# A pruned linear layer: seven tiles of x turned on TensorE instead of eight, the eighth's first half of K opened from natural weights and staged, weight pieces 2 and 3 by rows

## Chip, cores, metric

One core of a Trainium2 chip. The metric is the device time of one launch in microseconds, median over runs; the profile is of one further execution.

## The reference

x is 16 x 512 x 1024, w 1024 x 1024, b 1024, all bf16. Rows of w are taken in groups of four (M = 4), and in each group and column the two of the largest magnitude are kept (N = 2):

```python
wg = w.reshape(G, M, D)
mag = jnp.abs(wg)
order = jnp.argsort(mag, 1)
thr = jnp.take_along_axis(mag, order[:, M - N:M - N + 1, :], 1)
mask = (lambda x, dt: x.astype(dt))(mag >= thr, w.dtype)
wp = (wg * mask).reshape(D, D)
return jnp.einsum("bsd,df->bsf", x, wp) + b
```

## The kernel before

x is 8192 tokens, 64 tiles of 128 tokens (t = 0 to 63). K = 1024 is cut in two halves (g = 0, 1) of 512 rows. Output columns are cut in two halves (h) of FH = 512, and those in quarters (n) of CW = 256.

**Two layouts of the weights.** w is loaded with the four rows of a group side by side (`w_sb`: partition q, half g, row m of the group, column), since pruning compares those four. VectorE prunes it in six *pieces*: 0 to 3 are the four column quarters of the first half of K, 4 and 5 the two column halves of the second. Each piece goes through `abs`, `hi` and `lo` (maximum and minimum of two rows), `t1`, `t2`, `thr`, `mask` (L154) and `mult`, which writes `wp`. A letter behind a step cuts it: x and y are the row pairs m = 0, 1 and m = 2, 3; u, v, s, t are one m each. Pieces 0 and 1 are cut by rows in `mask` and `mult` (`halves`), 2 to 5 are whole. Once a column half of a K half is pruned, SBUF to SBUF DMAs (`spread`, token `W g.h`, four parts of 128 KB) write it in natural row order to `wp_nat`, which all later tiles use.

**Packed tiles.** While `wp_nat` isn't there yet, TensorE works on the first eight tiles (NPK = 8) with `wp` itself. The first half of K of each is loaded plainly (`load_x`, token rows interleaved by GROUPS), turned on TensorE with a stride of four (`transpose`, T tokens, four instructions of 128 x 128 each), copied to SBUF by ScalarE (`copy_xt`, C tokens) and multiplied in `mm_piece` (M t.piece, L216): 256 columns for one m. Two tiles share a PSUM bank per column quarter (`pairs`); ScalarE copies each full bank to a staging tile (`stage`, S tokens).

**Natural tiles.** All other tiles come by transposing DMAs: `load_lead` (X0, X1: the two K halves of tiles 8 to 11, LEAD = 4), `load_low` (Y1, Y0: the second K half of the packed tiles, in two groups of 384 and 640 rows) and `load_nat` (the batches of 4 and then 8 tiles, both K halves). They are multiplied in `nat` (L239): 512 columns for one of eight blocks kt of K. The lead tiles open with K blocks 0 to 3 (`open_nat`, A j h), and their PSUM banks are held until the second K half of the weights is there.

**Closes.** Then the list `closes` runs: for each (t, h), K blocks 4 to 7, an eviction on VectorE that adds the bias (L400) or the staged first half, to which GpSimd has added the bias (L402, L396), and a store when both halves are done. GpSimd's eight additions begin when the last piece is pruned. After the closes come 52 tiles of the main loop, 16 natural matmuls each.

**Order.** Every engine's instructions are chained in program order (`seq`), and up to the closes that order is written out by hand as four lists of tokens (`order`: pe, dve, act, sp). An engine thus stops at a token whose input is late, with all that stands behind it. PSUM has two banks for `tp` and six for `ps`. The fillers (F and the ones before) are matmuls on constants ahead of the first transposes.

Of the kernel before, what the change touches and what calls it, by code (L numbers as in the profile page):

```python
# [10 lines left out]
def kernel(  # L11
# [25 lines left out]
    xf = x.flatten_outer_dims()  # L37
    of = out.flatten_outer_dims()

    NPK = 8  # L40
    LEAD = 4
    GROUPS = ((0, 5), (5, 8))
    LATE = 5
    sizes = (4, 8, 8, 8, 8, 8, 8)
    batches = []
# [6 lines left out]
    const = ctx.enter_context(tc.tile_pool(name="const", bufs=1))  # L52
    wtmp = ctx.enter_context(tc.tile_pool(name="wtmp", bufs=1))
    xtp = ctx.enter_context(tc.tile_pool(name="xtp", bufs=NPK))
    stg = ctx.enter_context(tc.tile_pool(name="stg", bufs=NPK))
    xtb = ctx.enter_context(tc.tile_pool(name="xtb", bufs=2))
    outp = ctx.enter_context(tc.tile_pool(name="outp", bufs=10))
    psum_t = ctx.enter_context(tc.tile_pool(name="psum_t", bufs=2, space=bass.MemoryType.PSUM))
# [52 lines left out]
    load_w(0, 0, 256, 1, 2, "act")  # L111
    load_w(0, 0, 256, 2, 3)
    load_w(0, 0, 256, 3, 4, "act")
    load_x(7, 8, "act")
    load_x(0, 2, "act")
    act(nc.scalar.activation(spark[:], nc.const_aps.tensor(1.0, [P, 1], bf16), Act.Abs))
    load_x(5, 7)
    load_w(0, 256, 512)
    load_x(4, 5)
    load_x(2, 4)  # L120
    load_w(0, 512, 1024)
    load_w(1, 0, 512)
    sp(nc.sync.dma_start(bias_sb[:], b.partition_broadcast(P)))
    load_w(1, 512, 1024)
    pieces = [(0, 0, 256), (0, 256, 512), (0, 512, 768), (0, 768, 1024), (1, 0, 512), (1, 512, 1024)]

# [56 lines left out]

    def transpose(t):
        xg = x_sb[t].rearrange("p (q m) -> p m q", m=4)
        bank = psum_o.tile([P, FH], fp32, name="ps") if t == 6 else psum_t.tile([P, FH], fp32, name="tp")
        tp = bank[:].bitcast(bf16)[:, :FH].rearrange("p (m q) -> p m q", m=4)
        for m in range(4):
            pe(nc.tensor.transpose(tp[:, m, :], xg[:, m, :], ident[:]))  # L189
        xpk[t] = tp  # L190
# [7 lines left out]
    part = {"": slice(0, 4), "x": slice(0, 2), "y": slice(2, 4), "a": slice(0, 2), "b": slice(2, 4)}  # L198
    part.update({c: slice(m, m + 1) for m, c in enumerate("uvst")})
    half = {"a": slice(0, 1), "b": slice(1, 2)}  # L200
    pairs = [(5, 6), (0, 1), (2, 3), (4, 7)]
    pair_of = {t: q for q, pr in enumerate(pairs) for t in pr}
    left = {}

    def mm_piece(t, i, ms):
        g, c0, c1 = pieces[i]
        q, n = pair_of[t], c0 // CW
        new = (q, n) not in ps_open
        if new:
            ps_open[(q, n)] = psum_o.tile([P, FH], fp32, name="ps")  # L210
            left[(q, n)] = sum(8 for pc in pieces if pc[0] == 0 and pc[1] // CW == n)
        ps = ps_open[(q, n)]
        d = pairs[q].index(t) * CW - n * CW
        for m in range(ms.start, ms.stop):
            left[(q, n)] -= 1
            pe(nc.tensor.matmul(ps[:, c0 + d:c1 + d], lhsT=xpk[t][:, m, :],  # L216
                                rhs=wp[:, g, m, c0:c1],
                                start=(new and m == ms.start), stop=(left[(q, n)] == 0),
                                skip_group_check=True))

    xlead = const.tile([P, KT, LEAD * P], bf16)
# [15 lines left out]
    def nat(xt, ps, c0, c1, k0=0, k1=KT, first=0, last=KT - 1, koff=0):  # L237
        for kt in range(k0, k1):
            pe(nc.tensor.matmul(ps, lhsT=xt[:, kt - koff, :], rhs=wp_nat[:, kt, c0:c1],  # L239
                                start=(kt == first), stop=(kt == last)))  # L240

    def open_nat(j, h):
        t = NPK + j
        if j < 3:
            held[(t, h)] = psum_o.tile([P, FH], fp32, name="ps")
        else:
            held[(t, h)] = psum_t.tile([P, FH], fp32, name="tp")
        nat(xnat[t], held[(t, h)][:], h * FH, (h + 1) * FH, 0, 4)

    staged = {}  # L250

    def stage(q, n):
        if (q, n // 2) not in staged:
            staged[(q, n // 2)] = stg.tile([P, 2, 2, CW], fp32, name="st")
        st = staged[(q, n // 2)]
        act(nc.scalar.copy(st[:, n % 2, :, :].rearrange("p t c -> p (t c)"), ps_open.pop((q, n))[:]))  # L256

    order = {
        "pe": (
            "F8 T7a T5a T6a M7.0u M5.0u M7.0v M5.0v M6.0u M6.0v M7.0s M5.0s T1a M7.0t M5.0t M6.0t M6.0s "  # L260
            "T0a M1.0u M1.0v M1.0s M1.0t T4a T3a M0.0u M0.0v M0.0s M0.0t T2a M4.0u M4.0v M4.0s M4.0t "
            "M3.0u M3.0v M3.0s M3.0t M2.0u M2.0v M2.0s M2.0t M4.1x M5.1x M0.1x M7.1y M6.1y M2.1y M1.1y "
            "M3.1y M6.1x M4.1y M1.1x M3.1x M0.1y M7.1x M2.1x M5.1y M0.2 M3.2 M7.2 M1.2 M2.2 M4.2 M6.2 "
            "M0.3 M2.3 M5.3 M4.3 M5.2 M6.3 M3.3 M1.3 A0h0 A2h0 M7.3 A2h1 A1h0 A3h1 A0h1 A3h0 A1h1"
        ),
        "dve": (
            "abs0a hi0a abs0b lo0a lo0b hi0b t20 t10 thr0 mask0u mask0v mult0u mult0v mask0s mask0t mult0s mult0t abs1 lo1 hi1 "
            "t21 t11 thr1 mask1x mask1y mult1x mult1y abs2 hi2 lo2 t12 t22 thr2 mask2 mult2 hi3 lo3 "
            "t13 t23 thr3 mask3 mult3 abs5 abs4 hi4 lo4 t24 t14 thr4 mask4 mult4 hi5 lo5 t15 t25 "
            "thr5 mask5 mult5"  # L270
        ),
        "act": (
            "C7a C5a C6a C1a C0a C4a C3a C2a S3b0 S0b0 S1b0 S2b0 abs3 S3b1 S1b1 S0b1 S2b1 S2b2 S1b2 "
            "S3b2 S0b2 S1b3 S2b3 W1.0q S3b3 S0b3"
        ),
        "sp": (
            "W0.0 X0 X1 W0.1 Y1 W1.0p Y0 W1.1"
        ),
    }
    written = set()  # L280
    p = {}
    halves = {0: tuple("uvst"), 1: ('x', 'y')}

    by_rows = {0}

# [9 lines left out]
    def needs(eng, tok):  # L295
        base, k = split_tok(tok)
        if tok[0] == "C":
            return ["T" + tok[1:]]
        if tok[0] == "T":
            return ["C" + transposed[-2]] if tok != "T6a" and len(transposed) > 1 else []  # L300
        if tok[0] == "F":
            return []
        if tok[0] == "W":
            g, h = map(int, tok[1:4].split("."))
            return [n for i, pc in enumerate(pieces) if pc[0] == g and pc[1] // FH == h for n in all_of(f"mult{i}", i)]
        if tok[0] in "XY":
            return []
        if tok[0] == "A":
            return ["X0", f"W0.{tok.split('h')[1]}"]
        if base[0] == "M":  # L310
            t, i = base[1:].split(".")
            return [f"C{t}a", f"mult{i}{k}"]
        if tok[0] == "S":
            q, n = map(int, tok[1:].split("b"))
            return [f"M{t}.{x}" for i, pc in enumerate(pieces) if pc[0] == 0 and pc[1] // CW == n
                    for t in pairs[q] for x in all_of(str(i), i)]
        i, step = base[-1], base[:-1]
        before = {"abs": [], "hi": ["abs"], "lo": ["abs"], "t1": ["hi"], "t2": ["lo"],
                  "thr": ["t1", "t2"], "mask": ["thr", "hi", "lo"], "mult": ["mask"]}[step]
        out_ = []  # L320
        for b_ in before:
            if b_ in ("abs", "hi", "lo") and int(i) in by_rows:
                out_ += [b_ + i + k] if step in ("hi", "lo") else [b_ + i + s for s in "ab"]
            else:
                out_.append(b_ + i + (k if b_ == "mask" else ""))
        return out_

    def emit(eng, tok):
        base, k = split_tok(tok)
        if tok[0] == "T":  # L330
            transpose(int(tok[1:-1]))
            if tok != "T6a":
                transposed.append(tok[1:])
        elif tok[0] == "F":
            filler(int(tok[1:]))
# [4 lines left out]
            xnat.update(load_lead(int(tok[1:])))  # L340
        elif tok[0] == "Y":
            xnat.update(load_low(int(tok[1:])))
        elif tok[0] == "A":
            open_nat(*map(int, tok[1:].split("h")))
        elif tok[0] == "C":
            copy_xt(int(tok[1:-1]))
        elif tok[0] == "M":
            mm_piece(*map(int, base[1:].split(".")), part[k])
        elif tok[0] == "S":
            stage(*map(int, tok[1:].split("b")))  # L350
        else:
            i = int(base[-1])
            if i not in p:
                p[i] = Piece(i)
            if eng == "act":
                p[i].abs_act()
            else:
                p[i].do(base[:-1], part[k], half.get(k, slice(0, 2)))
# [27 lines left out]

    pruned = const.tile([P, 1], bf16)
    pool(nc.gpsimd.tensor_copy(out=pruned[:], in_=wp[:, 1, 3, Dout - 1:]))
    closes = [(8, 0), (9, 0), (10, 0), (11, 0), (5, 0), (6, 0), (7, 0), (8, 1), (9, 1), (10, 1), (11, 1), (5, 1), (6, 1), (7, 1), (4, 0), (4, 1), (0, 0), (0, 1), (1, 0), (1, 1), (2, 0), (2, 1), (3, 0), (3, 1)]
    done = set()  # L390
    for t, h in closes:
        if t < NPK and (pair_of[t], h) not in done:
            done.add((pair_of[t], h))
            st = staged[(pair_of[t], h)]
            bias = bias_sb[:, h * FH:(h + 1) * FH].rearrange("p (n c) -> p n c", n=2)
            pool(nc.gpsimd.tensor_tensor(st[:], st[:], bias[:, :, None, :].to_broadcast([P, 2, 2, CW]), op=Alu.add))  # L396

    def evac(o, ps, c0, c1, add=None):
        if add is None:
# [17 lines left out]
    def close(t, h):  # L417
# [2 lines left out]
        ps = held.pop((t, h), None)  # L420
        if ps is None:
            ps = psum_o.tile([P, FH], fp32, name="ps")
        nat(xnat[t], ps[:], h * FH, (h + 1) * FH, 4, 8, first=4 if t < NPK else 0, koff=4 if t < NPK else 0)
        add = None
        if t < NPK:
            add = staged[(pair_of[t], h)][:, :, pairs[pair_of[t]].index(t), :]
        evac(outs[t], ps[:], h * FH, (h + 1) * FH, add)
        closed[t] = closed.get(t, 0) + 1
        if closed[t] == 2:
# [61 lines left out]
```

## Time and profile before

| what | value |
|---|---|
| median of three runs | 233.23 us (233.18 to 233.81) |
| the profiled execution | 232.96 us, span 231.2 us |
| TensorE busy | 226.7 us (98%) |
| VectorE busy | 107.8 us (47%) |
| ScalarE, GpSimd busy | 13.5 us, 17.6 us |
| DMA | 38.19 MB, mean 165 GB/s |
| first transpose, first packed matmul | 4.95, 5.88 us after the span's start |
| first natural matmul | 20.68 us |
| first close | 28.03 us |

Times of instructions count from the start of the span; 1.8 us of the profiled execution lie around the span. PE is TensorE, PEld its weight loads, DVE VectorE, ACT ScalarE, POOL GpSimd, SP SyncE; a q behind an engine's name is its queue, where DMAs are issued. L numbers are lines of the kernel before. In a row with x2 or x4, consecutive instructions of one kind are merged, so its length runs from the first start to the last end. The end of a matmul is modelled, so starts are compared.

### The profile page before, as it was taken

The page shows a single profiled execution, that of the slowest core. Times are in us where ns is not written, and L with a number is a line of the kernel's source. Part 1 is how long each engine was busy: PE and PEld are TensorE (multiplying, and loading weights), DVE is VectorE, ACT ScalarE, POOL GpSimd, SP SyncE. Part 2 cuts the span into 40 slices and gives each one's busy share as a digit, 9 for nine tenths or more (in the row PEclk, how much of TensorE's full clock was granted, in tenths as well). Part 3 has the DMA queues.
Part 4 walks back from the last instruction along what each step waited for, and adds up shares of the span by engine and source line. Part 5 has one row for each costly group of instructions (what it writes and reads, how often), then busy time and mean ns, then how long its engine had stood idle before and what let it go on. Part 6 is the DMA issues. An engine that isn't in the chain of part 4 may idle for free.

```text
span 231.2 us, 2832 instructions
## 1 busy us (share of the span) xinstructions
PE 226.7 (98%) x1139; PEld 112.6 (49%) x1158; DVE 107.8 (47%) x188; ACT 13.5 (6%) x27; POOL 17.6 (8%) x15
## 2 busy tenths in 40 slices
PE   8999999999999999999999999999999999999995
PEld 5887444544444444444444444444444444444443
DVE  4999777844424424424424424424423423433434
ACT  3674100000000000000000000000000000000000
POOL 1000299600000000000000000000000000000000
DMA  6999999998499222991249821798129942122122
GB/s 195 357 218 236 228 165 250 265 203 252 183 221 261 110 91 66 244 281 61 78 122 237 231 94 68 167 190 238 67 91 188 247 155 84 55 91 87 57 86 91
DMA packets 78268, 38.19 MB, mean 165 GB/s; under 512 B 63664, under 2 KB 70576, under 8 KB 78256
## 3 DMA queue, kind: packets, MB, share of 16 engines
q1 hardware_dynamic: 67328, 20.61, 45.4%
q10 hardware_dynamic: 10928, 17.40, 21.9%
q8 instruction: 9, 0.15, 0.3%
q14 instruction: 3, 0.02, 0.0%
HBM read 3.41 MB, written 16.78 MB: 87 GB/s over the span
## 4 chain that ended last, share of the span: by engine, by line
PE 96%; DVE 1%; DMA 1%; issue 1%
PE ps L239 88%; PE ps L216 6%; PE tp L239 1%; DMA w_sb<-in_w_dram 1%; PE tp L189 0%; DVE hi L154 0%; DVE lo L154 0%; DVE mag L164 0%; DVE mag L154 0%; DVE o L400 0%; DVE wp L154 0%
## 5 line engine op out<-in xcount | busy, mean ns | idle before, releaser
L239 PE MATMUL ps<-wp_nat,xb 128*128 128x512 bf16 (+2 forms) x832 | 178.9, 375 | 0.8
L239 PEld LDWEIGHTS <-xb 128*128 128x128 bf16 x848 | 82.4, 98 | 97.5
L400 DVE TENSOR_TENSOR o<-ps,bias_sb 128x512 bf16<-128x512 f32 (+1 forms) x112 | 71.6, 677 | 114.2 <-PE ps L239 111.9
L396 POOL TENSOR_TENSOR st<-st,bias_sb 128x1024 f32<-128x1024 f32 x8 | 16.8, 2132 | 0.0
L216 PE MATMUL ps<-wp,xt 128*128 128x256 bf16 x128 | 15.1, 273 | 0.1
L239 PE MATMUL ps<-wp_nat,xlow 128*128 128x512 bf16 x62 | 14.0, 379 | 0.1
L216 PEld LDWEIGHTS <-xt 128*128 128x128 bf16 x128 | 12.2, 98 | 2.0 <-ACT xt L194 0.4
L402 DVE TENSOR_TENSOR o<-ps,st 128x512 bf16<-128x512 f32 x16 | 11.1, 692 | 2.8 <-PE ps L239 2.1
L239 PE MATMUL ps<-wp_nat,xlead 128*128 128x512 bf16 x47 | 11.1, 379 | 0.1
L239 PEld LDWEIGHTS <-xlow 128*128 128x128 bf16 x64 | 7.2, 112 | 6.7
L239 PEld LDWEIGHTS <-xlead 128*128 128x128 bf16 x64 | 6.3, 98 | 7.1
L256 ACT COPY st<-ps 128x512 f32<-128x512 f32 x16 | 8.4, 595 | 6.2 <-PE ps L216 3.7
L154 DVE TENSOR_TENSOR mag<-mag,hi 128x256 bf16<-128x256 bf16 (+3 forms) x10 | 5.6, 582 | 0.2
L154 DVE TENSOR_TENSOR wp<-w_sb,mag 128x256 bf16<-128x256 bf16 (+3 forms) x10 | 5.6, 581 | 0.1
L133 PE MATMUL ps<-const-bfloat16-1.0 128*128 128x128 bf16 (+1 forms) x22 | 4.3, 394 | 0.8 <-PEq L475 0.8
L239 PE MATMUL tp<-wp_nat,xlead 128*128 128x512 bf16 x16 | 4.1, 379 | 0.0
L164 DVE TENSOR_SCALAR mag<-w_sb 128x512 uint16<-128x512 uint16 (+2 forms) x6 | 2.7, 466 | 2.9 <-DMA w_sb<-in_w_dram 2.9
L133 PEld LDWEIGHTS <-const-bfloat16-1.0 128*128 128x128 bf16 x22 | 2.5, 148 | 2.4 <-issue 2.4
L154 DVE TENSOR_TENSOR hi<-mag 128x512 bf16<-128x512 bf16 (+2 forms) x7 | 3.2, 459 | 0.1
L154 DVE TENSOR_TENSOR lo<-mag 128x512 bf16<-128x512 bf16 (+2 forms) x7 | 3.1, 456 | 0.0
L194 ACT COPY xt<-tp 128x256 f32<-128x256 f32 x7 | 2.4, 375 | 3.1 <-PE tp L189 3.1
L189 PE MATMUL tp<-ident,x 128*128 128x128 bf16 x28 | 2.4, 219 | 0.0
(17 smaller groups left out, 14.1 us busy)
## 6 DMA issues: line engine op xcount, KB each, us to landing
out_dram<-o ACTq DMA_DIRECT2D x59, 256.0 KB, 2.5
wp_nat<-wp SPq DMA_DIRECT2D x14, 128.0 KB, 3.4
w_sb<-in_w_dram SPq DMA_DIRECT2D x3, 512.0 KB, 6.6
out_dram<-o ACTq DMA_DIRECT2D x8, 128.0 KB, 1.7
x<-in_x_dram SPq DMA_DIRECT2D x2, 256.0 KB, 4.0
w_sb<-in_w_dram SPq DMA_DIRECT2D x1, 256.0 KB, 4.6
x<-in_x_dram ACTq DMA_DIRECT2D x1, 256.0 KB, 3.7
bias_sb<-in_b_dram SPq DMA_DIRECT2D x1, 256.0 KB, 6.6
```

Source lines behind the costliest of these rows:

```text
L133: pe(nc.tensor.matmul(warm_ps[:, :rep * P], lhsT=nc.const_aps.tensor(1.0, [P, P], bf16), rhs=nc.const_aps.tensor(1.0, [P, rep * P], bf16), ...
L154: dve(nc.vector.tensor_tensor(out, a, b_, op=op))
L164: dve(nc.vector.tensor_single_scalar(self.mag[:, ms, :].bitcast(u16), self.w[:, ms, :].bitcast(u16), 0x7FFF, op=Alu.bitwise_and))
L189: pe(nc.tensor.transpose(tp[:, m, :], xg[:, m, :], ident[:]))
L194: act(nc.scalar.copy(xt[:].bitcast(fp32), xpk[t].bitcast(fp32)))
L216: pe(nc.tensor.matmul(ps[:, c0 + d:c1 + d], lhsT=xpk[t][:, m, :], rhs=wp[:, g, m, c0:c1], start=(new and m == ms.start), stop=(left[(q, n) ...
L239: pe(nc.tensor.matmul(ps, lhsT=xt[:, kt - koff, :], rhs=wp_nat[:, kt, c0:c1], start=(kt == first), stop=(kt == last)))
L256: act(nc.scalar.copy(st[:, n % 2, :, :].rearrange("p t c -> p (t c)"), ps_open.pop((q, n))[:]))
L396: pool(nc.gpsimd.tensor_tensor(st[:], st[:], bias[:, :, None, :].to_broadcast([P, 2, 2, CW]), op=Alu.add))
L400: dve(nc.vector.tensor_tensor(o[:, c0:c1], ps, bias_sb[:, c0:c1], op=Alu.add))
L402: dve(nc.vector.tensor_tensor(o[:, c0:c1].rearrange("p (n c) -> p n c", n=2), ps.rearrange("p (n c) -> p n c", n=2), add, op=Alu.add))
```

## The change

Seven tiles are packed (0 to 6), the lead has five (7 to 11), so the transposed loads X0 and X1 take 640 rows instead of 512, and the second halves of K come in groups of 512 (Y0) and 384 rows (Y1). Tile 7 is between the two kinds: its first half of K is opened with natural weights for each column half (E0, E1: `open_solo`, four natural matmuls into a `tp` bank), and staged by ScalarE (U7h0, U7h1); its close then goes like that of a packed tile. Tile 0 has no partner in a bank any more: it takes a bank of 512 columns for itself per column half (U0h0, U0h1), and shares its staging tile with tile 7. The number of staging copies (16) and of GpSimd's additions (8) stays.

The order is written anew for all four engines. On TensorE pieces 2 and 3 are taken by rows (2u, 2v, 2y; 3x, 3y), as VectorE now ends them, and E0 and E1 stand among the openings. On VectorE `abs5` comes after piece 4 and not before it. On SyncE the bias load moves from the initial loads to behind W0.1, W0.1 moves ahead of X1, and Y0 ahead of W1.1. Eight closes for column half 0 instead of seven precede the first for column half 1.

```diff
-    NPK = 8
-    LEAD = 4
-    GROUPS = ((0, 5), (5, 8))
+    NPK = 7
+    LEAD = 5
+    STG = 8
+    SOLO = 0
+    GROUPS = ((0, 4), (4, 7))
...
-    load_x(7, 8, "act")
-    load_x(0, 2, "act")
+    load_x(6, 7, "act")
+    load_x(0, 1, "act")
...
-    load_x(5, 7)
+    load_x(4, 6)
     load_w(0, 256, 512)
-    load_x(4, 5)
-    load_x(2, 4)
+    load_x(3, 4)
+    load_x(1, 3)
     load_w(0, 512, 1024)
     load_w(1, 0, 512)
-    sp(nc.sync.dma_start(bias_sb[:], b.partition_broadcast(P)))
     load_w(1, 512, 1024)
...
-    pairs = [(5, 6), (0, 1), (2, 3), (4, 7)]
+    pairs = [(4, 5), (SOLO, NPK), (1, 2), (3, 6)]
...
+        if t == SOLO:
+            key, d = (t, "h", c0 // FH), -(c0 // FH) * FH
+        else:
+            key, d = (q, n), pairs[q].index(t) * CW - n * CW
...
+    def open_solo(h):
+        ps = ps_open[(NPK, "h", h)] = psum_t.tile([P, FH], fp32, name="tp")
+        nat(xnat[NPK], ps[:], h * FH, (h + 1) * FH, 0, 4, last=3)
+
     def open_nat(j, h):
-        t = NPK + j
+        t = STG + j
...
-    def stage(q, n):
...
+    def stage(key):
+        solo = key[1] == "h"
+        q, h, at = (pair_of[key[0]], key[2], int(key[0] != SOLO)) if solo else (key[0], key[1] // 2, key[1] % 2)
...
         "pe": (
-            "F8 T7a T5a T6a M7.0u M5.0u M7.0v M5.0v M6.0u M6.0v M7.0s M5.0s T1a M7.0t M5.0t M6.0t M6.0s "
-            "T0a M1.0u M1.0v M1.0s M1.0t T4a T3a M0.0u M0.0v M0.0s M0.0t T2a M4.0u M4.0v M4.0s M4.0t "
-            "M3.0u M3.0v M3.0s M3.0t M2.0u M2.0v M2.0s M2.0t M4.1x M5.1x M0.1x M7.1y M6.1y M2.1y M1.1y "
-            "M3.1y M6.1x M4.1y M1.1x M3.1x M0.1y M7.1x M2.1x M5.1y M0.2 M3.2 M7.2 M1.2 M2.2 M4.2 M6.2 "
-            "M0.3 M2.3 M5.3 M4.3 M5.2 M6.3 M3.3 M1.3 A0h0 A2h0 M7.3 A2h1 A1h0 A3h1 A0h1 A3h0 A1h1"
+            "F8 T6a T4a T5a M6.0u M4.0u M6.0v M4.0v M5.0u M5.0v T0a M6.0s M4.0s M5.0s M6.0t T3a M4.0t M5.0t "
+            "M0.0s M0.0t T2a M3.0v T1a M3.0s M0.0v M0.0u M2.0t M2.0v M2.0u M3.0u M1.0t M1.0v M3.0t M2.0s "
+            "M1.0s M2.1x M3.1x M0.1x M6.1y M4.1y M1.0u M1.1y M2.1y M0.1y M4.1x M1.1x M5.1y M5.1x M6.1x M3.1y "
+            "M3.2u M2.2u M1.2u M6.2u M4.2u M5.2u M0.2u M3.2v M2.2v M1.2v M6.2v M4.2v M5.2v M0.2v M3.2y M2.2y "
+            "M1.2y M6.2y M4.2y M5.2y M0.2y M3.3x M6.3x M5.3x M1.3x M3.3y M6.3y M5.3y M1.3y M4.3x M4.3y M2.3x "
+            "M2.3y M0.3x M0.3y A0h0 E0 A2h0 A1h0 E1 A1h1 A3h0 A2h1 A3h1 A0h1"
         ),
         "dve": (
...
-            "t21 t11 thr1 mask1x mask1y mult1x mult1y abs2 hi2 lo2 t12 t22 thr2 mask2 mult2 hi3 lo3 "
-            "t13 t23 thr3 mask3 mult3 abs5 abs4 hi4 lo4 t24 t14 thr4 mask4 mult4 hi5 lo5 t15 t25 "
-            "thr5 mask5 mult5"
+            "mult0t abs1 lo1 hi1 t21 t11 thr1 mask1x mask1y mult1x mult1y abs2 lo2 hi2 t22 t12 thr2 mask2u "
+            "mask2v mult2u mult2v mask2y mult2y lo3 hi3 t23 t13 thr3 mask3x mult3x mask3y mult3y abs4 hi4 "
+            "lo4 t24 t14 thr4 mask4 mult4 abs5 lo5 hi5 t25 t15 thr5 mask5 mult5"
         ),
         "act": (
-            "C7a C5a C6a C1a C0a C4a C3a C2a S3b0 S0b0 S1b0 S2b0 abs3 S3b1 S1b1 S0b1 S2b1 S2b2 S1b2 "
-            "S3b2 S0b2 S1b3 S2b3 W1.0q S3b3 S0b3"
+            "C6a C4a C5a C0a C3a C2a C1a S3b0 abs3 S0b0 S2b0 U0h0 S2b1 S3b1 S0b1 S3b2 S2b2 S2b3 S0b2 S3b3 "
+            "S0b3 U0h1 U7h0 W1.0q U7h1"
         ),
         "sp": (
-            "W0.0 X0 X1 W0.1 Y1 W1.0p Y0 W1.1"
+            "W0.0 X0 W0.1 B X1 W1.0p Y1 Y0 W1.1"
         ),
...
-    halves = {0: tuple("uvst"), 1: ('x', 'y')}
+    halves = {0: tuple("uvst"), 1: ('x', 'y'), 2: ('u', 'v', 'y'), 3: ('x', 'y')}
...
-    closes = [(8, 0), (9, 0), (10, 0), (11, 0), (5, 0), (6, 0), (7, 0), (8, 1), (9, 1), (10, 1), (11, 1), (5, 1), (6, 1), (7, 1), (4, 0), (4, 1), (0, 0), (0, 1), (1, 0), (1, 1), (2, 0), (2, 1), (3, 0), (3, 1)]
+    closes = [(8, 0), (9, 0), (10, 0), (11, 0), (4, 0), (5, 0), (6, 0), (7, 0), (8, 1), (9, 1), (10, 1), (11, 1),
+              (4, 1), (5, 1), (6, 1), (7, 1), (3, 0), (3, 1), (0, 0), (0, 1), (1, 0), (1, 1), (2, 0), (2, 1)]
```

## The prediction

> **What bounds the kernel now.** I read the page first, then the chain of waits, then the timelines of VectorE and of SyncE's queue, then the tiles of the transposed x.
>
> ```profile
> span 231.2 us, 2832 instructions
> PE 226.7 (98%) x1139; PEld 112.6 (49%) x1158; DVE 107.8 (47%) x188; ACT 13.5 (6%) x27; POOL 17.6 (8%) x15
> ...
> PE 96%; DVE 1%; DMA 1%; issue 1%
> ```
>
> TensorE is busy for 98% and holds 96% of the chain. So time is won only by taking work or a wait from PE, and lost only where PE starts to wait. The chain in order of time (start, length, what):
>
> ```profile
> 5.88 1.19 PE ps L216 x8
> 7.07 0.22 PE tp L189 x4
> ...
> 9.49 11.35 PE ps L216 x104
> 20.85 1.08 PE ps L239 x5
> ...
> 27.33 3.45 PE ps L239 x16
> ```
>
> This gives three prices: a packed matmul (256 columns) 11.35/104 = 0.1092 us, one of the four transposes of a tile 0.0557 (0.22/4), a natural matmul (512 columns) 3.45/16 = 0.2157. From 5.88 to the end no other engine holds the chain for a quarter of a microsecond until the last stores. Inside the first row the eight matmuls start between 5.88 and 6.80, 0.92 us for seven steps of 0.109: gaps of 0.15 us in all, and that is all that PE loses before the natural matmuls. VectorE's timeline, which feeds it:
>
> ```profile
> 9.41 0.75 DVE L154 TENSOR_TENSOR wp<-w_sb,mag 128x512 bf16<-128x512 bf16 x2
> ...
> 12.78 0.69 DVE L154 TENSOR_TENSOR wp<-w_sb,mag 128x1024 bf16<-128x1024 bf16 x1
> ...
> 15.63 0.69 DVE L154 TENSOR_TENSOR wp<-w_sb,mag 128x1024 bf16<-128x1024 bf16 x1
> 16.24 1.29 DVE L164 TENSOR_SCALAR mag<-w_sb 128x2048 uint16<-128x2048 uint16 x2
> ...
> 26.26 1.23 DVE L154 TENSOR_TENSOR wp<-w_sb,mag 128x2048 bf16<-128x2048 bf16 x1
> ```
>
> These are the multiplications that end pieces 1, 2, 3 and the last one (5), and the two absolute values between. SyncE's queue:
>
> ```profile
> 10.19 2.55 SPq L98 DMA_DIRECT2D wp_nat<-wp  x4
> 12.78 4.91 SPq L224 DMA_TRANSPOSE xlead<-in_x_dram  x2
> 17.79 2.49 SPq L98 DMA_DIRECT2D wp_nat<-wp  x4
> ...
> 27.54 3.38 SPq L98 DMA_DIRECT2D wp_nat<-wp  x4
> ```
>
> They are W0.0, X0 and X1, W0.1, and W1.1. And the two tiles, with time from issue to landing:
>
> ```profile
> L224 SPq DMA_TRANSPOSE xlead<-in_x_dram x2: 1628/2430/3233, 12.8 to 16.1; - x2
> ...
> DMA to landing us min/median/max: 4.4/5.0/5.6
> ```
>
> ```profile
> L231 SPq DMA_TRANSPOSE xlow<-in_x_dram x2: 1571/2558/3545, 20.3 to 23.9; - x2
> ...
> DMA to landing us min/median/max: 3.8/5.5/7.1
> ```
>
> X0 (the 5.6) lands at 18.4 and PE wants it at 20.68, the start of its first natural matmul. The 3.5 us and the 7.1 belong to the one transfer of 640 rows.
>
> **PE's work.** Removed: four transposes, 4 x 0.0557 = 0.22, and 16 packed matmuls of the eighth tile, 16 x 0.1092 = 1.75. Added: E0 and E1, 8 natural matmuls, 8 x 0.2157 = 1.73. Sum -0.24 us, all on the path. The bank waits at the start stay: the same three tiles are transposed first, and piece 0 is made by the same instructions.
>
> **PE against VectorE.** From 5.88 come 27 packed matmuls, four transposed tiles (0.22 each) and some 0.10 of start gaps: PE asks for piece 1 at 9.82. Its first half is ready at 9.83, so PE waits some 0.05 there, which uses up what is left of the old 0.15. The third x tile to be transposed late (T3a, at 7.29) needs a load that landed at 7.38 before; 128 KB less of x goes ahead of it, at the 316 to 359 GB/s of those microseconds 0.36 us, so 7.0. If not, 0.1 is lost. Piece 2 is asked for at 9.87 + 29 x 0.1092 = 13.04. By rows its mask and product come as 256 columns for one m: starts 0.21 apart (the row of piece 0, 0.49 for two), so the first product ends at 12.05 + 0.21 x 2 + 0.29 = 12.75. Slack 0.29. Piece 3 is asked for at 13.04 + 28 x 0.1092 = 16.10. Rows cost VectorE some 0.15 more here, yet the half product ends at 16.05 instead of the whole at 16.33: slack 0.05, the whole split being needed. The second half ends at 16.84, asked for at 16.97. So the last packed matmul ends at about 19.2, 1.5 us earlier than PE turned to natural weights before (it has 16 fewer of them in front).
>
> **The transfers now needed earlier.** W0.0 is released by piece 1 as before (10.19) and lands at 16.2: no wait. X0 follows at 12.78 with 640 rows for 512: 128 rows are 131 KB, at the 269 GB/s of that stretch 0.49 us, so it lands at 18.4 + 0.5 = 18.9, while PE wants it at 19.1 to 19.2. That is the thinnest cover of the change, 0.3 us for 2.3 before. The row for the price is X0's own, since it has the same place in the queue; the queue ahead is emptier (256 KB of bias and 128 KB of x are gone from it). Low bound 18.0 (the emptier queue wins 0.9, what W0.0's last part stood behind), high bound 12.78 + 7.1 = 19.9 (the 640 rows of xlow).
>
> W0.1 waits for the end of piece 3, 16.84 for 16.33, but no longer stands behind X1: issue 16.9 to 19.4, landing 2.4 later as before, 21.8. E1, placed fifth, wants its first part at 19.2 + 4 x 0.863 = 22.65. Slack 0.8. The bias now follows W0.1 (0.6 on the queue); it lands by 26 with its old 6.6 us, and its first reader, an eviction after the first close or GpSimd's addition, comes after 28. X1 goes behind it at 20.1; with 7.1 it lands at 27.2, wanted at 27.84. W1.0's first half stands behind X1 on SP; piece 4 ends 0.1 earlier (16.76 for 16.84 at its start, nothing between), it lands at some 26.5 to 27.5, wanted from 27.84 to 28.5.
>
> Piece 5 loses the absolute value that ran in piece 4's shadow: its 0.6 is now in its own chain, so its product ends at 27.49 + 0.63 = 28.1. Behind it are W1.1 and GpSimd's eight additions. W1.1: 28.15 + 3.4 = 31.5 at the last issue, landing 2.3 later, 33.9; its fourth part is wanted at 27.84 + 8 x 0.863 + 0.65 = 35.4, because eight closes precede it now instead of seven. GpSimd's first addition ends at 30.4 and each next 2.13 later; the third, which closes tile 7's half, ends at 34.7, just when that close ends. It delays one eviction, no matmul. The staging of E0 on ScalarE (0.6) lies beside A2h0, and A3h0 asks for its bank 2 us later; U7h1 stands behind W1.0's issue on ScalarE's queue (22.6 + 1.64), done at 24.9, asked for at 26.1.
>
> **Sum.** -0.24 for work, 0 for waits: the profiled execution of 232.96 (span 231.2 and 1.8 around it) becomes 232.7. The three runs have a median 0.27 higher, 233.23, so I predict 233.0 for a median. Since PE has nothing else to shed, a gain of more than 0.4 us (0.24 and the 0.15 of gaps) is not in the profile.
>
> **Rivals.** About 0.3%, 0.7 us, is what a measurement of this kernel tells from no change; its three runs already lie that far apart.
>
> *Small waits eat the gain.* For it: slack 0.05 at pieces 1 and 3, and 0.3 at X0. Against it: each is only as long as its miss. With X0 at its bound of 19.9, PE waits 0.8, and the time is 233.23 - 0.24 + 0.8 = 233.8; with 0.1 to 0.3 lost at the pieces, 233.2. Still within the bound. Chance 0.18.
>
> *X0 comes late enough to make it slower.* PE turns to natural weights with nothing left to fill the hole. It decides from a landing of 20.1 on (19.15 + 0.24 + 0.7). For it: X0 is the first transposed transfer, whose issue took 3.2 for X1's 1.6; if that 1.6 comes on top of the 3.5 of 640 rows, issue ends at 17.9 and landing, 3.6 after as with xlow, is 21.5: a wait of 2.35 and 235.3. Against it: xlow's 640 rows stood behind W1.0 from two queues, X0's queue is emptier than before. Chance 0.10.
>
> *W1.1 comes late.* Y0 now stands ahead of it on SP and VectorE ends 0.6 later. If Y0 takes the 3.5 us issue from 25.5, W1.1's last issue ends at 32.5, and with the longest landing of a part (5.0 for 2.9) at 36.9: a wait of 1.5, 234.5. Slack of 1.5 on the likely rows speaks against it. Chance 0.05.
>
> *The clock falls.* The 22 filler matmuls took 4.34 us for 40 blocks of 128 columns, 0.108 each; the transposes right behind them, 128 columns too, 0.0557. PE thus starts at half its rate and is let go at about 4.9 (the granted clock reads 1.00 in every stretch, so it is the spacing that tells). A hole long enough to bring that back would cost its own length and the matmuls after it at twice their price: with 3.4 idle and 3.4 at half rate 3.4 + 1.7 - 0.24, 238.1. The rows show no hole, and my far bound for X0 is 2.35. Chance 0.02. The Trainium skill (TensorE: Matmul & The Clock Gate, Part 1: The HAM clock gate) says that the clock halves after one idle window of about 3.4 us and needs as long to come back; by that rule the X0 rival alone does not trigger it.
>
> *Faster by over 0.3%* would need PE's first product earlier than 5.88, and the four first weight loads that gate it are untouched: 0.03.
>
> **How the numbers follow.** Forecast 0.62, within the bound; small waits 0.18, within it too: same 0.80. Slower 0.10 + 0.05 + 0.02 = 0.17, faster 0.03. The range goes from 232.6 (all gaps closed) to 234.2, which holds X0's bound of 233.8 and the nearer part of the late cases; the clock, half of the late ones and a little below are left out.
>
> **What would show it.** Right: the chain goes from packed matmuls to the first natural ones at about 19.2 without a PE wait, X0 lands at or before that, and the first close starts at 27.8 instead of 28.03; the rest is the same length. Wrong: a PE gap before the first matmul on xlead (X0), at the fifth group (W0.1), at pieces 2 and 3 (VectorE), or at the ninth close (W1.1); or an end that moves by more than the first close does.

## The result

The changed kernel has a median of 233.98 us against 233.23; the ratio is 1.0024 (95% interval 1.0015 to 1.0033), so it is slower by some 0.56 us, within the 0.3% that I called no change, but outside what its own interval allows for no change. (The ratio lies near the quotient of the means, 1.0025; the quotient of the medians is 1.0032.) In a later session (e11 below) the ratio was 1.0031 (1.0020 to 1.0042). One execution of e6 was a slow one, 239.56 us at a granted clock of 0.993 where all others show 0.999 or more, and e6's median is that of the other ten. I had forecast 0.24 us less. The profiled execution took 234.06 us with a span of 232.3.

The page after, first lines and engine shares of the chain:

```profile
span 232.3 us, 2832 instructions
PE 227.3 (98%) x1146; PEld 110.8 (48%) x1146; DVE 108.5 (47%) x194; ACT 13.1 (6%) x26; POOL 17.6 (8%) x15
...
PE 93%; DMA 3%; SPq 1%; DVE 0%; issue 0%; ACT 0%
```

Before, DMA held 1% of the chain (the chain is the work that ended last, followed back from the end) and SyncE's queue none; now they hold 4%. The chain in order of time shows where, first at the start:

```profile
1.65 4.44 DMA x<-in_x_dram
...
6.14 0.43 PE tp L190 x4
6.56 0.02 issue
6.59 0.38 ACT xt L195
6.97 0.05 issue
7.01 0.72 PE ps L220 x5
```

then, with nothing but PE between, at the ninth close:

```profile
30.60 0.70 DVE o L426
31.30 0.05 SPq L100
31.35 0.04 issue
31.39 1.41 SPq L100
32.81 0.04 issue
32.85 0.60 SPq L100
33.46 0.04 issue
33.50 3.14 DMA wp_nat<-wp
36.64 0.04 issue
36.68 2.10 PE ps L243 x9
```

The first part is a late load of two x tiles: the second packed matmul starts at 7.01 for 6.08 before. The second part is W1.1: its last part lands at 36.64, and PE, which wanted it at 36.22, waits 0.46. The DVE row is an eviction, which W1.1 does not read; what W1.1 stood behind is seen in SyncE's queue:

```profile
10.47 3.38 SPq L100 DMA_DIRECT2D wp_nat<-wp  x4
13.90 2.58 SPq L228 DMA_TRANSPOSE xlead<-in_x_dram  x1
17.17 2.81 SPq L100 DMA_DIRECT2D wp_nat<-wp  x4
20.03 0.60 SPq L361 DMA_DIRECT2D bias_sb<-in_b_dram  x1
20.68 4.49 SPq L228 DMA_TRANSPOSE xlead<-in_x_dram  x1
25.26 1.20 SPq L100 DMA_DIRECT2D wp_nat<-wp  x2
26.50 4.21 SPq L235 DMA_TRANSPOSE xlow<-in_x_dram  x2
30.81 3.29 SPq L100 DMA_DIRECT2D wp_nat<-wp  x4
```

These rows are W0.0, X0, W0.1, the bias, X1, half of W1.0, Y1 with Y0, and W1.1. X1, right behind the bias load, occupies the queue for 4.49 us (X1 before, of 512 rows: 1.63). So W1.0's half goes out at 25.26, though piece 4 ended at 22.86, and W1.1 at 30.81, right behind Y0 (28.00 to 30.71), though piece 5 ended at 28.43 as the last row of VectorE's timeline shows:

```profile
27.21 1.23 DVE L155 TENSOR_TENSOR wp<-w_sb,mag 128x2048 bf16<-128x2048 bf16 x1
```

### The profile page after: what moved, and what is told of

Its sections match the earlier page's. It is cut to its first block, busy times and chain, and to the rows that moved or that the text cites. A ratio compares the mean times of both kernels' runs of the same rounds, so it can differ in the third digit from the quotient of the medians.

```text
span 232.3 us, 2832 instructions
## 1 busy us (share of the span) xinstructions
PE 227.3 (98%) x1146; PEld 110.8 (48%) x1146; DVE 108.5 (47%) x194; ACT 13.1 (6%) x26; POOL 17.6 (8%) x15
## 4 chain that ended last, share of the span: by engine, by line
PE 93%; DMA 3%; SPq 1%; DVE 0%; issue 0%; ACT 0%
PE ps L243 86%; PE ps L220 5%; DMA x<-in_x_dram 2%; PE tp L243 2%; DMA wp_nat<-wp 1%; SPq L100 1%; PE tp L190 1%; DVE o L426 0%; ACT xt L195 0%
## 5 line engine op out<-in xcount | busy, mean ns | idle before, releaser
L243 PE MATMUL ps<-wp_nat,xlead 128*128 128x512 bf16 x56 | 13.4, 379 | 0.3 <-DMA wp_nat<-wp 0.3
L220 PE MATMUL ps<-wp,xt 128*128 128x256 bf16 x112 | 13.2, 273 | 0.1
L243 PE MATMUL ps<-wp_nat,xlow 128*128 128x512 bf16 x56 | 12.6, 379 | 0.0
L243 PEld LDWEIGHTS <-xlead 128*128 128x128 bf16 x80 | 7.8, 98 | 9.7 <-issue 0.6
L220 PEld LDWEIGHTS <-xt 128*128 128x128 bf16 x112 | 10.7, 98 | 1.6 <-ACT xt L195 0.4
L265 ACT COPY st<-ps 128x512 f32<-128x512 f32 x14 | 7.2, 598 | 4.2 <-PE ps L220 4.2
L243 PE MATMUL tp<-wp_nat,xlead 128*128 128x512 bf16 x24 | 6.2, 379 | 0.0
L155 DVE TENSOR_TENSOR mag<-mag,hi 128x256 bf16<-128x256 bf16 (+2 forms) x13 | 6.0, 484 | 0.2
L155 DVE TENSOR_TENSOR wp<-w_sb,mag 128x256 bf16<-128x256 bf16 (+2 forms) x13 | 5.9, 483 | 0.2
L190 PEld LDWEIGHTS <-x 128*128 128x128 bf16 x28 | 2.1, 114 | 1.4 <-DMA x<-in_x_dram 1.4
```

What stands on the lines that cost most here:

```text
L155: dve(nc.vector.tensor_tensor(out, a, b_, op=op))
L265: act(nc.scalar.copy(staged[(q, h)][:, at, :, :].rearrange("p t c -> p (t c)"), ps_open.pop(key)[:]))
```

## The experiments

Theories: *Queue* (the loss is W1.1, behind a bias load that slows X1 and behind Y0), against *Stride* (tokens of a group of four are read in steps of 8 KB, which would make the first x tiles late), and, for the later runs, *Edge* (X0 lands too late by a few tenths), *Floor* (W1.1's landing sets the changed kernel's end, whatever is won ahead of it) and *Start* (the late start belongs to the change). All were timed in five rounds; ratios are to the kernel before on the same chip in the same session (medians 233.34 for e1 to e4, 233.36 for e5 to e8, 233.28 for e9 to e12), so runs of different sessions are compared by their ratios.

**e1: the bias load early again**

```diff
+    sp(nc.sync.dma_start(bias_sb[:], b.partition_broadcast(P)))
     load_w(1, 512, 1024)
-            "W0.0 X0 W0.1 B X1 W1.0p Y1 Y0 W1.1"
+            "W0.0 X0 W0.1 X1 W1.0p Y1 Y0 W1.1"
```

> The changed kernel with the bias load back among the initial loads. Theory Bias (its 128 row copies behind W0.1 slow X1 from some 2.4 to 4.3 us of packets, and W1.0, Y1, Y0 and W1.1 move behind): X1's issue takes at most 3.6 us instead of 4.5, W1.1's last part lands before 36.0, the wait of 0.46 at the ninth close goes, 0.3 to 0.5 us less than the changed kernel (some 233.5). Rival Order (Y0 ahead of W1.1 does it alone): the wait stays, within 0.1 us of the changed kernel. The late start (first transpose at 5.6 for 4.95) stays under both.

233.32 us, ratio 1.0009 (0.9998 to 1.0019). By the ratios it is 0.35 us below the changed kernel (0.5 below e11), as expected; the medians, of two sessions, differ by 0.66. The queue in this run:

```profile
20.80 2.99 SPq L229 DMA_TRANSPOSE xlead<-in_x_dram  x1
23.89 1.52 SPq L100 DMA_DIRECT2D wp_nat<-wp  x2
25.46 4.62 SPq L236 DMA_TRANSPOSE xlow<-in_x_dram  x2
30.18 3.01 SPq L100 DMA_DIRECT2D wp_nat<-wp  x4
```

X1's issue took 2.99 for 4.49, W1.1's last part landed at 35.64 and PE didn't wait at the ninth close. But Y0 still holds W1.1 back to 30.18, and the gain of work does not show: in this profile PE waited 0.53 at T3a, the second x tile transposed late, whose x landed at 8.11, and 0.07 at T2a behind it (8.86).

```profile
2.94 5.16 DMA x<-in_x_dram
8.11 0.05 issue
8.15 0.41 PE tp L191 x4
```

**e2, e3: groups of one and six tiles, without and with the early bias load**

```diff
-    GROUPS = ((0, 4), (4, 7))
+    GROUPS = ((0, 1), (1, 7))
```

> The changed kernel with the packed tiles grouped 1 and 6 instead of 4 and 3, so that no plain load of x takes every fourth token row (steps of 8 KB). Theory Stride (rows 8 KB apart load slower and hold up the first x tiles): first packed matmul at 5.9 to 6.1 instead of 6.6, 0.6 to 0.8 us less than the changed kernel (some 233.3). Rival Chance (the start varies from run to run for any grouping): median within 0.2 us of the changed kernel (233.8 to 234.1). The wait at the ninth close may shrink by some 0.3 as Y0 is 128 rows here.

> Both edits of the two runs before. Bias and Stride together: no wait left, first packed matmul at about 5.9, 0.25 us below the kernel before, 232.9 to 233.1. If Chance is right for the start: 233.4 to 233.6. If Order is right for the close: as the run with the grouping alone.

e2: 234.60 us, ratio 1.0061 (1.0048 to 1.0074), slower than either kernel. The start was early (second packed matmul at 6.30), but Y1, now 768 rows and behind the slowed X1, landed at 33.0 and PE waited 1.24 us for it. e3: 233.52, ratio 1.0008 (0.9999 to 1.0017), with the start late (6.77). So the early bias load is worth 1.1 us in this grouping. The x tiles that are turned first do not land by the stride: at 5.21 and 5.40 in e1, with groups of four, at 5.22 and 5.41 in e3.

**e4: groups of four in the kernel before**

```diff
-    GROUPS = ((0, 5), (5, 8))
+    GROUPS = ((0, 4), (4, 8))
```

> The kernel before with groups of 4 and 4 tiles instead of 5 and 3, so that all its plain loads of x take every fourth token row; nothing else changed but the two transposed loads of 512 and 512 rows. Stride: first packed matmul 0.5 to 0.9 us later, 233.8 to 234.2. Chance: within 0.2 us of the kernel before, 233.0 to 233.4.

233.12 us, ratio 0.9998 (0.9990 to 1.0007), with a profile that happened to start late (6.92, time 233.81). Stride falls. The start varies from execution to execution: over the fourteen profiles of this study, that of the kernel before among them, the second packed matmul starts between 6.08 and 7.01, and the kernel before's own profile is the earliest of all. Two different things make it late. In the changed kernel's profile and in e11 the x tiles land late: 5.47 and 6.09, 5.66 and 5.87, where the others have 4.8 to 5.5. In e3, e4 and e12 they land at 5.1 to 5.4, but PE still runs at half its rate. First e4, then e11:

```profile
1.66 3.70 DMA x<-in_x_dram
...
5.41 1.04 PE tp L189 x8
```

```profile
1.67 4.00 DMA x<-in_x_dram
...
5.71 0.67 PE tp L190 x8
```

The twelve first transposes start 0.107 apart in e3, e4 and e12, up to 6.2 to 6.7, as the fillers of 128 columns do at the beginning; in the other profiles they are 0.056 apart from 5.5 at the latest, but for what they wait for. In e7 the fillers themselves are 0.06 apart from 3.5 on. So the half rate ends at 3.5 to 6.7 us, differently from execution to execution.

**e5, e6: W1.1 ahead of Y0, with the bias load early (e5) and late (e6)**

```diff
-            "W0.0 X0 W0.1 B X1 W1.0p Y1 Y0 W1.1"
+            "W0.0 X0 W0.1 X1 W1.0p Y1 W1.1 Y0"
```

> The changed kernel with the bias load back among the initial loads and W1.1 ahead of Y0 on SyncE's queue. Theory Queue (all that the change loses against its -0.24 of work is W1.1, which stands behind the slowed X1, Y1 and Y0): W1.1's first part issued within 0.2 us of piece 5's end (28.3 to 28.8), its last lands by 34.5, no PE wait after the first packed matmuls, median 0.15 to 0.3 us below the kernel before (ratio 0.9987 to 0.9994). Rival Start (the loss sits in x tiles that land later than before, for reasons of the new loads): as with the bias load alone, 0.0 to 0.2 us above the kernel before.

> The changed kernel with W1.1 ahead of Y0 only, the bias load still behind W0.1. Queue: the wait at the ninth close goes; what is left are X1 and W1.0 behind the bias load, which land at 28.2 to 28.8 and are wanted from 27.8 where the start is early, a wait of 0.1 to 0.4; 0.4 to 0.6 us less than the changed kernel, 233.2 to 233.5. Theory Bias alone (the order of Y0 and W1.1 does nothing): within 0.15 us of the changed kernel, 233.8 to 234.1.

e5: 233.64, ratio 1.0013 (0.9999 to 1.0027). W1.1 went out at 28.47 and landed at 33.56, as expected, and yet the median isn't below the kernel before: the chain shows the next wait, X0.

```profile
14.06 5.66 DMA xlead<-in_x_dram
19.71 0.04 issue
19.76 1.04 PE ps L244 x4
```

X0 landed at 19.71 and PE stood 0.27 us before its first natural matmul. e6: 233.71, ratio 1.0016 (1.0002 to 1.0030); no wait at the ninth close (W1.1 at 34.18), 0.19 for X0, 0.16 and 0.10 earlier. It is more than expected: by the ratios the order of Y0 and W1.1 is worth 0.2 us (0.35 against e11) with the bias load late, which is not clear of the intervals, though the wait for W1.1 itself is gone.

**e7: the kernel before with only the bias load moved behind W0.1**

```diff
-    sp(nc.sync.dma_start(bias_sb[:], b.partition_broadcast(P)))
     load_w(1, 512, 1024)
-            "W0.0 X0 X1 W0.1 Y1 W1.0p Y0 W1.1"
+            "W0.0 X0 X1 W0.1 B Y1 W1.0p Y0 W1.1"
```

> The kernel before with only the bias load moved behind W0.1. Queue: the row copies slow what follows them (Y1 and W1.0's first half) by up to 2 us; W1.0 landed at 27.1 and was wanted at 28.0 to 28.7, so a wait of 0 to 1 us at the first close: 233.2 to 234.2, with the bias load landing more than 3.5 us after its issue again. Rival: the bias load costs only beside a transposed load of 640 rows; Y1 has 384 here, and the time is within 0.15 us of the kernel before.

233.66, ratio 1.0014 (1.0000 to 1.0027): moving the bias load costs the kernel before some 0.3 us by itself, with an interval from 0 to 0.6. Its chain ends as the changed kernel's does:

```profile
26.12 3.47 SPq L230
...
33.37 2.95 DMA wp_nat<-wp
36.32 0.04 issue
36.36 2.10 PE ps L238 x9
```

In this profile PE waited 0.33 at the first close and 0.50 at the first close of the second column half. It is the slowest of the twelve executions (234.61): the weights of piece 1 landed only at 7.92 (6.70 in the profile before), which put VectorE's pieces from there on behind, and PE had waited 0.36 for an x tile as well. So it shows where the queue binds, but its waits are not the 0.3 of the median.

**e8: as e5, with piece 5's absolute value ahead of piece 4's**

```diff
-            "mask2v mult2u mult2v mask2y mult2y lo3 hi3 t23 t13 thr3 mask3x mult3x mask3y mult3y abs4 hi4 "
-            "lo4 t24 t14 thr4 mask4 mult4 abs5 lo5 hi5 t25 t15 thr5 mask5 mult5"
+            "mask2v mult2u mult2v mask2y mult2y lo3 hi3 t23 t13 thr3 mask3x mult3x mask3y mult3y abs5 abs4 hi4 "
+            "lo4 t24 t14 thr4 mask4 mult4 lo5 hi5 t25 t15 thr5 mask5 mult5"
```

> As the kernel with the bias load early and W1.1 ahead of Y0, with the absolute value of piece 5 ahead of piece 4's again, as before the change. Queue: both orders have cover (W1.1 lands 0.6 earlier, W1.0 0.6 later, at 27.5 to 28), so within 0.15 us of that kernel. If piece 5's later end is what limits: 0.2 to 0.5 us less. If W1.0 has no cover: 0.2 to 0.5 us more, with a PE wait at the first close.

233.33, ratio 1.0001 (0.9989 to 1.0012). Its interval overlaps with e5's, so the edit's own worth stays open. Its profile is the clean case, with no wait of PE after the second packed matmul:

```profile
6.15 0.99 PE ps L221 x6
7.14 0.22 PE tp L191 x4
7.37 0.44 PE ps L221 x4
...
9.02 10.59 PE ps L221 x97
19.61 0.86 PE ps L244 x4
```

That execution took 233.01 us, the least of the eleven. From the second packed matmul (6.42) to the last matmul (228.36) are 221.94 us, for 222.22 in the profile before (6.08 to 228.30), of which 0.06 was a gap. So 0.22 us of work is gone, where 0.24 was worked out.

**e9, e10, e12: X0 ahead of W0.0.** e9 is e8 with that edit, e12 is e5 with it, e10 is the changed kernel with it:

```diff
-            "W0.0 X0 W0.1 B X1 W1.0p Y1 Y0 W1.1"
+            "X0 W0.0 W0.1 B X1 W1.0p Y1 Y0 W1.1"
```

> Bias load early, W1.1 ahead of Y0, piece 5's absolute value ahead of piece 4's, and X0 ahead of W0.0 on SyncE's queue. In the runs so far X0 landed at 19.2 to 20.1, within 0.3 us of PE's first natural matmul or after it. Theory Edge (in executions with an early start PE waits there for X0): X0 lands before 18.5, no wait at the first natural matmul in any execution, median 0.1 to 0.3 us below the kernel before (ratio 0.9987 to 0.9996). Rival Jitter (only the start of the plain loads scatters the times; X0 costs nothing on the median): same median as without the edit, ratio 0.9995 to 1.0005; slower if W0.0, now behind X0, lands after 19.2.

> The changed kernel with X0 ahead of W0.0 and nothing else. Theory Floor (W1.1, behind bias load, X1 and Y0, ends last, so that what comes before it can't help): within 0.15 us of the changed kernel, with a PE wait at the ninth close of 0.4 to 1.2 us, the longer the earlier the start. Rival (X0 is what the changed kernel loses by): 0.3 us or more less than the changed kernel.

> As the kernel with all four edits, but piece 5's absolute value stays behind piece 4. If only queue order mattered: within 0.1 us of that kernel. If piece 5's end 0.6 us later still limits: a PE wait at the ninth close or at GpSimd's additions, 0.1 to 0.4 us more.

e9: 233.64, ratio 1.0016 (1.0003 to 1.0029); e12: 233.54, ratio 1.0014 (1.0003 to 1.0026). X0 landed at 18.28 and 18.52, so no wait for it, but what Edge hoped for is not there: W0.0, now behind X0, left SyncE only at 14.9 to 15.1 and landed at 20.50 and 20.64, so that PE waited 0.26 and 0.21 for its last part; in e9 T2a waited 0.35 too. The two runs differ in the order of `abs4` and `abs5` alone, and their ratios hardly, as the first branch of e12's expectation had it.

e10: 233.87, ratio 1.0024 (1.0013 to 1.0034): X0 three microseconds earlier is worth nothing to the changed kernel, as Floor expects. Its chain:

```profile
33.36 3.21 DMA wp_nat<-wp
36.56 0.04 issue
36.61 2.10 PE ps L243 x9
```

**e11: the changed kernel again**

> The changed kernel once more, on one chip with the others. Floor: 233.7 to 234.1, a PE wait at the ninth close of 0.4 to 1.2 us in the profile, and if the first packed matmuls start at 6.1 to 6.4 (the late 6.6 to 7.0 of its first profile was chance) a wait longer than 0.46. Rival Start (the late start belongs to the changed kernel): the second packed matmul again at 6.9 or later.

233.90. The start was late once more (6.89, the sign that I had named for Start), and the wait at the ninth close only 0.10, less than expected, as the late start takes it up. But e10 and e6 have the same plain loads, which land at 5.0 to 5.4 there, and start at 6.31 and 6.43; so I take the late start for chance, on four profiles, two of them late. Put beside each other, the three profiles with the changed kernel's queue behind W0.1 give the floor: from the landing of W1.1's last part to the last matmul's start are 229.40 - 36.64 = 192.76 us in the first, 229.07 - 36.31 = 192.76 in e11, 229.33 - 36.56 = 192.77 in e10, whatever the start. That is the least there can be, so W1.1 sets the end in all three. In e1 the same stretch has 0.7 to spare (229.10 - 35.64), in e8 1.8, in e5 2.4.

| run | median | ratio to before | wait for W1.1 in its profile |
|---|---|---|---|
| changed | 233.98 | 1.0024 | 0.46 |
| e11 changed again | 233.90 | 1.0031 | 0.10 |
| e10 + X0 first | 233.87 | 1.0024 | 0.54 |
| e6 + W1.1 before Y0 | 233.71 | 1.0016 | 0 |
| e1 + bias early | 233.32 | 1.0009 | 0 |
| e5 + both | 233.64 | 1.0013 | 0 |
| e8 + both, abs5 first | 233.33 | 1.0001 | 0 |

No version here beats the kernel before beyond its interval.

## Why the prediction was wrong

**The work was right.** -0.24 us was worked out; e8's profile shows -0.22, and PE's waits in the profiles account for each of the others to within some hundredths. The first natural matmul, worked out at 19.1 to 19.2, starts there at 19.45, with a start 0.34 later than the one that I counted from.

**The step that failed is the cover of W1.1**, in "The transfers now needed earlier". I had its first part go out as soon as piece 5 ends, at 28.15, and its last land at 33.9, wanted at 35.4. It landed at 36.3 to 36.6. Piece 5 itself was near (28.4 for 28.1, the start being 0.3 late). The 2.7 us come from the issue, 30.8 for 28.15, and two terms carry them:

- The bias load was costed as "0.6 on the queue". The issue is 0.60, but its 128 row copies overlap with X1's on the DMA engines. Early in the kernel they took 92 ns each (mean of 128 in the profile before); behind W0.1, 168 ns with single ones up to 613, and X1's 2560 copies of 256 bytes took 4.3 us from first to last, where X0's took 3.0 in the same profile and X1's 3.1 in e1. So X1's issue was 4.49, and everything behind moved. Whether the form of the load or only its size does this was not tried: at X1's rate in e1 (655 KB in 3.1 us) the 262 KB of the bias load would take 1.2 us, an estimate that is all of the difference. Undone alone (e1), that gives back most of the loss; done alone to the kernel before (e7), it costs some 0.3 us, with an interval from 0.
- Y0 ahead of W1.1. I had priced it as a rival ("if Y0 takes the 3.5 us issue from 25.5"), with its chance at 0.05, because I let Y0 start at 25.5. That start comes out of W1.0's half right behind piece 4, at about 22.6, and Y1's 1.6 after it, and leaves X1 at most 2.5 us of issue from 20.1. Y0 began at 28.0, the bias and X1 having moved it, and kept W1.1 back to 30.8. Putting W1.1 first (e6) takes the wait away too, even with the bias load late.

So the mechanism of the slower side stood in the text, and what was wrong is that I added up the queue by the issue times of an emptier one. X1's issue took 1.63 us before (512 rows), 2.99 in e1 and 4.49 in the changed kernel, by what stood ahead of it. The row of xlow, 3.54 us for 640 rows, had hinted at that; I took its 7.1 for X1's landing (20.1 + 7.1 = 27.2) and not its 3.54 for the queue behind X1.

**The rivals.** X0 landed 5.6 to 6.5 us after its issue began, where I took 6.1. But its issue began at 12.9 to 14.5 and not at 12.78, in most profiles because the issue of a part of W0.0 took 1.2 to 1.6 us for 0.6; so the cover of 0.3 was gone in e5 and e6, where PE waited 0.27 and 0.19, and the 0.5 to 0.6 to spare in the changed kernel's two profiles are owed to their late start. It does not decide the changed kernel (e10). The small waits at pieces 1 to 3 were 0.03 to 0.10 where they came. The clock rival did not occur: the longest hole was 1.24 us, in e2, and no run here tests the rule. That PE is let go at about 4.9, which I read from one profile, holds for that profile; in e3, e4 and e12 it was 6.2 to 6.7.

**A cover that was mis-sized.** For T3a (the second x tile transposed late, which I called the third) I had its x land at 7.0, wanted at 7.29, and 0.1 lost if not. In the runs with seven packed tiles it landed at 7.1 to 8.1, and PE waited 0.53 in e1, 0.16 in e6 and 0.17 in e10. T2a behind it I did not work out. With one packed tile fewer in front, it comes 1.87 us after the second packed matmul, and the transpose that needs the same load 2.37 before; its x lands at 7.9 to 8.9, and PE waited 0.35 in e9 and 0.12 in e11. An early start can thus be partly given back, the more easily in the changed kernel; e7, with its 0.36, shows that the kernel before is not free of it.

**The median.** I took the profile before as an ordinary execution, and its 0.27 to the median as unexplained. Its start is the earliest of fourteen, by 0.17 us (6.08, then 6.25 in e9); a start as late as most of the others' would make up the 0.27, though the unprofiled executions don't show theirs.

**What stays open.** e5 and e8 have no wait for W1.1 and 0.22 us less work, and yet ratios of 1.0013 and 1.0001. The profiles show waits for X0, for the tiles of T3a and T2a and, in e9 and e12, W0.0, each in some executions, and starts that PE's half rate made late; how much each takes from the median was not separated. Whether e8's order of absolute values did anything stays open too: e8 against e5 (0.3 us, intervals overlapping) speaks for it, e9 against e12 (none) does not. Why the bias row copies are slow beside a transposed load was not tried either; that they are, the packets show.

## What to carry to other kernels

When PE is the bound and its work shrinks by a quarter of a microsecond, ask of every transfer on the path's queue how much cover is left, and sum the queue by what its transfers take behind the traffic that will be there, not by the issue times of an emptier stretch. A load taken from an idle stretch to a busy one is not free because its issue is short. And only profiles of several executions tell whether a late start belongs to the kernel; whether the tiles landed late or PE's rate rose late is told by the spacing of the first transposes.

## What was not expected of the hardware

- A load of one 2 KB row to 128 partitions took 6.6 us to land among the initial loads without harm, and 4.3 to 4.7 behind W0.1, where its copies had a mean of 114 to 168 ns for 92 and X1's issue behind it took 4.0 to 4.5 us for 2.6 to 3.5 without it (e1, e3, e5, e8). Early, but with X0's transposed load right behind it (e9, e12), its copies had a mean of 213 and 166 ns.
- With the same initial loads in the same order (the changed kernel, e6, e10, e11) the first transpose starts at 5.00 to 5.71. PE's half rate at the beginning (matmuls of 128 columns 0.107 us apart, then 0.056) ended at 3.5 us in e7 and at 6.7 in e4, after the same fillers from 0.75 on.
- An instruction fetch of 16 KB appears among the DMA packets near 12.5 and again near 31.5 us, each taking 0.96 us in the changed kernel; the issue of a part of W0.0 and of W1.1 beside it took 1.4 us for 0.6.
